# The issue order of all engines, read from a table, in a fused decay-attention and two-MLP kernel

## Chip, cores and metric

One NeuronCore of a Trainium2 chip runs the whole program. The metric is device time in microseconds (us) of one execution, of which the profile's span is the part from the first to the last instruction; durations of single instructions are in nanoseconds (ns).

## What is computed

Inputs are `q`, `k`, `v` of shape (2, 8, 768, 64), one decay `lam` for each of 8 heads, and five weight matrices. The reference, cut to what matters:

```python
for b in range(nb):                                   # blocks of 64 positions
    intra = (qb @ kb.T * Dmask) @ vb
    inter = (qb * lam_pow) @ kv_state
    out[b] = intra + inter
    kv_state = lam**64 * kv_state + (kb * rev_pow).T @ vb
x = out.transpose(0, 2, 1, 3).reshape(1536, 512)
x = (sigmoid(x @ w_gate) * (x @ w_val)) @ w_out       # 512 -> 1536 -> 512
h = x @ w_in                                          # 512 -> 2048
g = where(h > 0, h, exp(min(h, 0)) - 1)
return g @ w_out2                                     # 2048 -> 512
```

## The kernel before

The sequence is cut into 6 chunks of 128 positions. The 1536 tokens stand as columns, in a set of 512 (two chunks of both batches) and one of 1024; the hidden widths are worked off in slices of 256, six of them in the first MLP and eight in the second. Nothing is run in the order of the code: every call on an engine is recorded as an operation (`record`, L167; L182 is the line where all of them are issued later, so every row of the profile has L182), `hazards` (L207) finds which operations must precede which, and `issue` (L408) then chooses one order of all 4713 recorded entries and issues them in it. Each engine runs its own queue strictly in that order and waits on semaphores where a hazard crosses engines.

The order before comes from a list scheduler. `cost` (L140) gives each operation a duration, `run` (L271) simulates the five engines, forwards and backwards, with several settings, and `exchange` (L385) joins the best stages of the orders found; `mark` (L368) sets the stage bounds.

The products are made with operands split in a high and a low part (`h` and `l` in names), three matmuls for each pair of tiles, in fp32r. `product` (L657) makes the 512-row products of a slice in Strassen's manner: seven block products M2, M5, M1, M4, M3, M7, M6 of six matmuls each, in three PSUM banks. M4 and M7 use the first bank one after the other, M3 and M6 the second, so the first matmul of M7 must wait until the result of M4 has been read out of the bank by ScalarE (a sigmoid or an exponential) or VectorE (a multiplication by the gate). The moving operand has 256 columns for the first token set and 512 for the second. `unit` (L996) and `wino_units` (L973) make the output products of a slice in chains in two banks, each followed by an addition into the accumulator by VectorE (`adder`, L1007). `scores` (L788) and the chunk loop make the attention out of groups of small matmuls on 64 by 64 tiles (`together`, L190); the first products of the first MLP are put between these groups.

The profile names a PSUM bank by its first user: `warm` is the bank A0, `direct` B0, `st` one of A1, B1, C0, C1, and `xu` or `x` one of the two banks of the output products. `w` are weights while they are unpacked and split by ScalarE, VectorE and GpSimd.

Of the kernel before, what the change touches and what calls it, by code (L numbers as in the profile page):

```python
# [19 lines left out]
P = 128  # L20
B, H, S, D = 2, 8, 768, 64
# [15 lines left out]
WORDS = 4096  # L37

# [89 lines left out]
class Work:  # L128
# [6 lines left out]
    def __init__(self, nc):  # L135
        self.nc, self.ops, self.block, self.marks = nc, [], None, [0]
        for name in ENGINES:
            setattr(self, name, Engine(self, name))

    def cost(self, op, fn, args, kw):  # L140
# [13 lines left out]
        if fn == "dma_start":  # L154
            return 440, n * P * 4 / 423 if op.eng == "sync" else 2000
# [115 lines left out]
    def run(self, preds, key, backward=False, gate=None, stick=0, thrift=20000):  # L271
        ops = self.ops[::-1] if backward else self.ops
        n = len(ops)
        after, left = [[] for _ in range(n)], [len(p) for p in preds]
        for k, p in enumerate(preds):
            for x in p:
                after[x].append(k)
        ripe, soon = {e: [] for e in ENGINES}, {e: [] for e in ENGINES}
        at, start, end = [max(0.0, g) for g in gate] if gate else [0.0] * n, [0.0] * n, [0.0] * n
        free = dict.fromkeys(ENGINES, 0.0)  # L280
        port = behind = 0.0
        queue = 3500.0
        shape = table = None
        told, pages = 0, {}

        def stall(op, t, keep=False):
            late = 0.0
            here = {}
            for m in range((told + self.FIRST) // self.PAGE, (told + op.words + self.FIRST + self.LEAD) // self.PAGE + 1):
                for mark in (m * self.PAGE - self.FIRST - self.LEAD, m * self.PAGE - self.FIRST):  # L290
                    if m < 2 or not told <= mark < told + op.words:
                        continue
                    now = t + late + op.gap * (mark - told) / op.words
                    if mark == m * self.PAGE - self.FIRST:
                        late += max(0.0, here.get(m, pages.get(m, 0)) - now)
                    else:
                        here[m] = now + (self.SLOW if queue > now + 2000 else self.FAST)
            if keep:
                pages.update(here)
            return late  # L300

        for k in range(n):
            if not left[k]:
                heapq.heappush(soon[ops[k].eng], (at[k], k))
        for _ in range(sum(op.eng is not None for op in ops)):
            t, e = min((free[e] if ripe[e] else max(free[e], soon[e][0][0]), i, e)
                       for i, e in enumerate(ENGINES) if ripe[e] or soon[e])[::2]
            while soon[e] and soon[e][0][0] <= t:
                k = heapq.heappop(soon[e])[1]
                heapq.heappush(ripe[e], (key[k], k))  # L310
            rank, k = heapq.heappop(ripe[e])
            if e == "tensor" and stick and ops[k].shape != shape:
                like = min((x for x in ripe[e] if x[0] < rank + stick and ops[x[1]].shape == shape), default=None)
                if like:
                    ripe[e].remove(like)
                    heapq.heapify(ripe[e])
                    heapq.heappush(ripe[e], (rank, k))
                    k = like[1]
            if e == "tensor" and not backward and thrift and stall(ops[k], t) > 100:
                like = min((x for x in ripe[e] if x[0] < rank + thrift and not stall(ops[x[1]], t)), default=None,  # L320
                           key=lambda x: (ops[x[1]].words, x))
                if like:
                    ripe[e].remove(like)
                    heapq.heapify(ripe[e])
                    heapq.heappush(ripe[e], (rank, k))
                    k = like[1]
            op = ops[k]
            if e == "sync":
                late = 300 if queue < t + 2000 or t < 3000 else 1100
                queue = max(t + 2000, queue) + op.took  # L330
                free[e], end[k] = t + op.gap, queue + late
            elif e == "tensor":
                t += 60 if t > free[e] + 1 else 0
                t += self.SWITCH if op.shape != shape else 0
                shape = op.shape
                late = 0.0
                if not backward:
                    late = stall(op, t, True)
                    told += op.words
                free[e], end[k] = t + late + op.gap, t + late + op.took  # L340
            else:
                if op.table and op.table != table:
                    t, table = t + self.TABLE, op.table
                go = max(t, port, behind if e == "gpsimd" else 0) if op.port else t
                free[e], end[k] = go + op.gap, go + op.took
                if op.port:
                    port = free[e]
                    behind = end[k] + self.HANDOFF["gpsimd"] if e == "vector" else 0
            start[k] = t
            done = [k]  # L350
            while done:
                x = done.pop()
                for s in after[x]:
                    f = ops[s].eng
                    near = e == "tensor" or e == "sync" and (ops[s].prev is op or op.prev is ops[s])
                    ready = free[e] if f == e and x == k and near else end[x] + self.HANDOFF.get(f, 0)
                    at[s] = max(at[s], ready)
                    left[s] -= 1
                    if left[s]:
                        continue  # L360
                    if f is None:
                        start[s] = end[s] = at[s]
                        done.append(s)
                    else:
                        heapq.heappush(soon[f], (at[s], s))
        return start, end

    def mark(self):  # L368
        self.marks.append(len(self.ops))

    def clocks(self, plans):
        work = [sum(op.gap for op in self.ops[:m] if op.eng == "tensor") for m in self.marks[1:]]
        clocks = []
        for start, end in plans:
            order = sorted((start[k], op.gap) for k, op in enumerate(self.ops) if op.eng == "tensor")
            at, done, clock = 0, 0.0, [0.0]
            for w in work:
                while done + order[at][1] <= w:
                    done += order[at][1]
                    at += 1  # L380
                clock.append(order[at][0] + w - done)
            clocks.append(clock + [max(end)])
        return clocks

    def exchange(self, preds, plans, tries=8):  # L385
        bounds = self.marks + [len(self.ops)]
        best = min(plans, key=lambda x: max(x[1]))
        for i in list(range(len(self.marks))) * 2:
            clocks = self.clocks(plans)
            mine = self.clocks([best])[0]  # L390
            ranked = sorted(range(len(plans)), key=lambda r: clocks[r][i + 1] - clocks[r][i])
            for r in ranked[:tries]:
                gain = mine[i + 1] - mine[i] - clocks[r][i + 1] + clocks[r][i]
                if gain <= 0:
                    break
                key = list(best[0])
                for k in range(bounds[i], bounds[i + 1]):
                    key[k] = plans[r][0][k] - clocks[r][i] + mine[i]
                for k in range(bounds[i + 1], len(self.ops)):
                    key[k] -= gain  # L400
                made = self.run(preds, key)
                plans.append(made)
                if max(made[1]) < max(best[1]):
                    best = made
                    mine = self.clocks([best])[0]
        return best

    def issue(self, tc, rounds=7):  # L408
        self.hazards()
        n = len(self.ops)  # L410
        preds = [op.preds for op in self.ops]
        turned = [[] for _ in range(n)]
        for k, p in enumerate(preds):
            for x in p:
                turned[n - 1 - x].append(n - 1 - k)
# [33 lines left out]
def tile_decay_attention_two_mlps(  # L449
# [314 lines left out]
    n = 1  # L764
# [309 lines left out]
    for i in range(1, NG1):  # L1074
# [3 lines left out]
        if i in (2, NG1 - 1):  # L1078
            work.mark()
# [118 lines left out]
```

## Time and profile before

| | before |
|---|---|
| median of 3 runs (lowest, highest) | 581.99 us (581.05, 582.67) |
| the profiled execution's own time | 581.52 us |
| its span, first to last instruction | 579.6 us |
| PE busy | 569.1 us, 98% of the span, 3998 matmuls |
| VectorE busy | 447.8 us, 77%, 771 instructions |
| GpSimd busy | 317.2 us, 55% |
| ScalarE busy | 312.6 us, 54% |
| granted TensorE clock | 0.999 |
| moved by DMA | 52.03 MB, 90 GB/s |

The stages of the span are: to about 71 us the attention with the first products between its groups, to 300 us the first MLP, to 360 us its last slice and the split of its result into the operands of the second, to 520 us the second MLP, and then its last outputs. A row of the timeline gives start, duration, engine, operation and operands; in brackets is the idle time before it and what ended it.

### The profile page before, as it was taken

The page shows a single profiled execution, that of the slowest core. Times are in us where ns is not written, and L with a number is a line of the kernel's source. Part 1 is how long each engine was busy: PE and PEld are TensorE (multiplying, and loading weights), DVE is VectorE, ACT ScalarE, POOL GpSimd, SP SyncE. Part 2 cuts the span into 40 slices and gives each one's busy share as a digit, 9 for nine tenths or more (in the row PEclk, how much of TensorE's full clock was granted, in tenths as well). Part 3 has the DMA queues.
Part 4 walks back from the last instruction along what each step waited for, and adds up shares of the span by engine and source line. Part 5 has one row for each costly group of instructions (what it writes and reads, how often), then busy time and mean ns, then how long its engine had stood idle before and what let it go on. Part 6 is the DMA issues. An engine that isn't in the chain of part 4 may idle for free.

```text
span 579.6 us, 10208 instructions
## 1 busy us (share of the span) xinstructions
PE 569.1 (98%) x3998; PEld 487.2 (84%) x3998; DVE 447.8 (77%) x771; ACT 312.6 (54%) x612; POOL 317.2 (55%) x273
## 2 busy tenths in 40 slices
PE   7899999999999999999999999999999999999997
PEld 4788898888888888888898888888888888888886
DVE  6877844679999989989978994777676667686484
ACT  4893656445345345444457887764746554735160
POOL 2677678875365555553688865574738180712100
PEclk9999999999999999999999999999999999999999
DMA  8946211221221211210140222232222222200014
GB/s 298 411 168 219 75 74 74 74 74 72 74 73 67 80 47 73 98 55 21 72 146 2 74 73 74 72 144 76 73 74 72 74 74 73 74 0 1 0 37 181
DMA packets 10271, 52.03 MB, mean 90 GB/s; under 512 B 1264, under 2 KB 1520, under 8 KB 5744
## 3 DMA queue, kind: packets, MB, share of 16 engines
q1 hardware_dynamic: 10224, 51.39, 24.4%
q8 instruction: 31, 0.51, 0.3%
q14 instruction: 16, 0.13, 0.1%
HBM read 48.24 MB, written 3.15 MB: 89 GB/s over the span
## 4 chain that ended last, share of the span: by engine, by line
PE 89%; ACT 4%; DVE 3%; DMA 3%; issue 1%; SPq 0%; POOL 0%; ACTq 0%; DVEq 0%
PE xu L182 35%; PE st L182 32%; PE direct L182 10%; PE warm L182 9%; PE x L182 2%; DMA w<-in_w_val 1%; DMA w<-in_w_gate 1%; ACT kd L182 1%; ACT w L182 1%; DVE sig L182 1%; DVE sums L182 1%; DVE gl L182 0%; DVE xu L182 0%; ACT sig L182 0%; ACT x143h L182 0%
## 5 line engine op out<-in xcount | busy, mean ns | idle before, releaser
L182 DVE TENSOR_TENSOR acc<-xu,acc 128x512 f32<-128x512 f32 x144 | 96.8, 684 | 21.7 <-PE xu L182 20.9
L182 POOL TENSOR_TENSOR t<-w 128x256 f32<-128x256 f32 (+1 forms) x80 | 69.3, 887 | 70.2 <-DVE w L182 57.6
L182 PE MATMUL xu<-gl,woh 128*128 128x512 f32 (+1 forms) x274 | 107.2, 391 | 0.1
L182 PE MATMUL xu<-gh,woh 128*128 128x512 f32 (+1 forms) x274 | 106.9, 394 | 0.3 <-DVE xt L182 0.2
L182 PE MATMUL xu<-gh,wol 128*128 128x512 f32 (+1 forms) x274 | 106.5, 389 | 0.0
L182 POOL TENSOR_TENSOR wol<-w,woh 128x512 fp32r<-128x512 f32 x34 | 43.4, 1294 | 67.2 <-ACT woh L182 66.5
L182 POOL TENSOR_TENSOR gl<-sig,gh 128x512 fp32r<-128x512 f32 (+1 forms) x30 | 55.0, 1844 | 40.0 <-ACT gh L182 23.9
L182 POOL TENSOR_TENSOR l<-t,h 128x768 fp32r<-128x768 f32 (+1 forms) x38 | 62.6, 1654 | 13.0 <-ACT h L182 4.9
L182 ACT CAST gh<-sig 128x512 fp32r<-128x512 f32 (+1 forms) x66 | 46.7, 714 | 32.5 <-DVE sig L182 31.6
L182 PEld LDWEIGHTS xu<-gh,woh 128*128 128x128 f32 x274 | 51.4, 188 | 11.3 <-DVE xt L182 0.8
L182 PEld LDWEIGHTS xu<-gh,wol 128*128 128x128 f32 x274 | 51.5, 188 | 10.4
L182 PEld LDWEIGHTS xu<-gl,woh 128*128 128x128 f32 x274 | 51.5, 188 | 10.0 <-DVE gl L182 0.5
L182 ACT ACTIVATE sig<-st 128x512 f32<-128x512 f32 (+1 forms) x52 | 29.2, 566 | 53.4 <-PE st L182 35.5
L182 DVE SCALAR_TENSOR_TENSOR w<-w,w 128x1024 uint32<-128x1024 uint32 (+1 forms) x36 | 54.0, 1503 | 0.3
L182 PE MATMUL st<-x143l,h 128*128 128x512 f32 (+1 forms) x150 | 51.8, 347 | 0.0
L182 PE MATMUL st<-x143h,h 128*128 128x512 f32 (+1 forms) x150 | 51.3, 347 | 0.0
L182 PE MATMUL st<-x143h,l 128*128 128x512 f32 (+1 forms) x150 | 50.7, 347 | 0.0
L182 ACT ACTIVATE w<-w 128x1024 f32<-128x1024 f32 (+1 forms) x36 | 39.3, 1092 | 18.0 <-POOL l L182 10.5
L182 DVE TENSOR_SCALAR w<-w 128x1024 uint32<-128x1024 uint32 (+1 forms) x36 | 32.2, 896 | 18.8 <-ACT w L182 18.6
L182 DVE TENSOR_TENSOR wt<-st,wt 128x512 f32<-128x512 f32 (+1 forms) x57 | 31.5, 556 | 14.2 <-PE st L182 13.9
L182 ACT CAST h<-t 128x768 fp32r<-128x768 f32 (+1 forms) x40 | 29.1, 727 | 13.0 <-POOL t L182 12.8
L182 ACT ACTIVATE sig<-sig 128x256 f32<-128x256 f32 (+1 forms) x68 | 34.2, 510 | 1.3
(190 smaller groups left out, 1495.3 us busy)
## 6 DMA issues: line engine op xcount, KB each, us to landing
w<-in_w_out SPq DMA_DIRECT2D x14, 1024.0 KB, 4.8
w<-in_w_in SPq DMA_DIRECT2D x8, 1024.0 KB, 4.8
nat<-in_att SPq DMA_DIRECT2D x12, 512.0 KB, 9.9
w<-in_w_gate SPq DMA_DIRECT2D x5, 1024.0 KB, 4.8
w<-in_w_val SPq DMA_DIRECT2D x5, 1024.0 KB, 4.8
tin<-in_att SPq DMA_DIRECT2D x6, 512.0 KB, 9.7
tin<-in_att SPq DMA_DIRECT2D x3, 1024.0 KB, 11.4
out_t<-o SPq DMA_DIRECT2D x11, 256.0 KB, 2.0
```

Source lines behind the costliest of these rows:

```text
L182: return [getattr(getattr(self.nc, eng), fn)(*(real(a) for a in args), **{k: real(a) for k, a in kw.items()})]
```

## The change

The search leaves the kernel. In its place stands the order that a search elsewhere has found, as a table: one number for each recorded entry, packed as text, from which `order` takes the place of every entry and sorts. It asserts that no entry stands ahead of one that it depends on. The recorded operations, their operands, tiles, buffers and hazards are the same; the two numbers changed in `cost` for a DMA set nothing that is issued any more. Of the 23 KB of table two lines are shown.

```diff
-import heapq
+import base64
 import re
+import zlib
...
+ORDER_TABLE = (
+    'c-qZad2pRqb-(-aZEw?ilAg6$a%4M>qr?u5?O=ywASJOOw6)tp2d0@erDcXv+UdB{q=6yrv>hlNngV~MftJve0FxnGlN3V2V(=u8#WpzgZp*'
...
+    'G<f4Yx4gm=?T3'
+)
...
-            return 440, n * P * 4 / 423 if op.eng == "sync" else 2000
+            return 500, n * P * 4 / 410 if op.eng == "sync" else 2000
...
-    def run(self, preds, key, backward=False, gate=None, stick=0, thrift=20000):
...
-    def exchange(self, preds, plans, tries=8):
...
-    def issue(self, tc, rounds=7):
+    def order(self):
+        raw = np.frombuffer(zlib.decompress(base64.b85decode("".join(ORDER_TABLE))), np.uint8)
+        steps = np.ascontiguousarray(raw.reshape(2, -1).T).view("<i2")[:, 0].astype(int)
+        places = np.cumsum(steps) + np.arange(len(steps))
+        assert len(places) == len(self.ops), "the table is of another program"
+        assert all(places[p] < places[k] for k, op in enumerate(self.ops) for p in op.preds), "an order against a hazard"
+        return np.argsort(places).tolist()
+
+    def issue(self, tc):
         self.hazards()
...
-        order = sorted(range(n), key=lambda k: (best[1][k], k))
+        order = self.order()
```

Counted over the whole program: the 71 transfers stand in the same order on the SP queue. On PE, of 2892 fp32r matmuls, a 512-column one is followed by a 256-column one 129 times where it was 154, and as often the other way round. The small-matmul groups of the attention are entered from, or left to, other matmuls less often: from a group back to fp32r matmuls 14 times where it was 17. Pieces of one product or chain that stand together are 873 where they were 804, and 310 of them are a single matmul where 160 were. VectorE, ScalarE and GpSimd get other orders throughout. Three places follow; before the change a call's line is L182, after it L228, and numbers at names are those of buffers.

PE, early in the attention: `st<-tin` are score groups, `warm<-x11h,h` the first two fp32r matmuls of the first product. Before:

```order
L182 MATMUL st<-tin 64x2x64
L182 MATMUL st<-tin 64x64 x4
L182 MATMUL warm<-x11h,h_180 128x256 x2
L182 MATMUL st<-tin 64x128
L182 MATMUL st<-tin 64x2x64
```

With the change:

```order
L228 MATMUL st<-tin 64x2x64
L228 MATMUL st<-tin 64x64 x4
L228 MATMUL st<-tin 64x128
L228 MATMUL st<-tin 64x2x64
L228 MATMUL st<-tin 64x128
```

The two matmuls of the product have moved behind the second group.

PE, in the third slice of the first MLP, a product of the value weights with 256 columns: M3 in the bank `direct`, then M7 in `warm`, then M6 in `direct` again, which needs the result of M3 read out. Before:

```order
L182 MATMUL direct_494<-x143h0_330,l11_474 128x256
L182 MATMUL warm_80<-xPh0_513,h3_593 128x256
L182 MATMUL warm_80<-xPl0_544,h3_593 128x256
L182 MATMUL warm_80<-xPh0_513,l3_612 128x256
L182 MATMUL warm_80<-xPh0_513,h3_593 128x256
L182 MATMUL warm_80<-xPl0_544,h3_593 128x256
L182 MATMUL warm_80<-xPh0_513,l3_612 128x256
L182 MATMUL st_147<-x143l1_454,h3_593 128x512
L182 MATMUL direct_494<-xPh0_513,h3_593 128x256
```

With the change:

```order
L228 MATMUL direct_516<-x143h0_425,l11_449 128x256
L228 MATMUL warm_79<-xPh0_451,h3_518 128x256
L228 MATMUL warm_79<-xPl0_646,h3_518 128x256
L228 MATMUL warm_79<-xPh0_451,l3_543 128x256
L228 MATMUL warm_79<-xPh0_451,h3_518 128x256
L228 MATMUL warm_79<-xPl0_646,h3_518 128x256
L228 MATMUL warm_79<-xPh0_451,l3_543 128x256
L228 MATMUL direct_516<-xPh0_451,h3_518 128x256
```

The 512-column matmul of another product (`st`) no longer stands between M7 and M6.

VectorE, in the last slice of the first MLP: `sig<-warm,sig` multiplies M7 by the gate and frees the bank `warm` for the next product. Before:

```order
L182 TENSOR_TENSOR sig_1511<-direct,sig_1511 128x256
L182 TENSOR_TENSOR warm<-warm,wt_1042 128x256
L182 TENSOR_SCALAR w_163<-w_163 128x1024
L182 TENSOR_TENSOR xu<-xu,acc_1400 128x512
L182 TENSOR_TENSOR sig_1511<-warm,sig_1511 128x256
```

With the change:

```order
L228 TENSOR_TENSOR xt<-xu,acc_1406 128x256
L228 TENSOR_TENSOR xu<-xu,acc_1406 128x512
L228 TENSOR_TENSOR warm<-warm,wt_1078 128x256
L228 TENSOR_TENSOR sig_1455<-warm,sig_1455 128x256
L228 TENSOR_TENSOR sums<-xu,acc_1406 128x256
```

The unpacking of weights and the addition to `xu` no longer stand between the two steps of M7.

## Rows read from the trace of the kernel before

**Rows 1.** The page: busy us, share of the span, instructions.
```profile
PE 569.1 (98%) x3998; PEld 487.2 (84%) x3998; DVE 447.8 (77%) x771; ACT 312.6 (54%) x612; POOL 317.2 (55%) x273
```
**Rows 2.** Busy time by stage: us, PE, PEld, DVE, ACT, POOL, PEclk, DMA, GB/s.
```profile
90.00:300.00 210.00, 209.90 (x1164) 182.57 (x1163) 183.00 (x279) 95.66 (x167) 124.72 (x111) 1.00 0.20 71
360.00:520.00 160.00, 160.00 (x804) 134.76 (x804) 114.18 (x181) 91.56 (x163) 83.98 (x68) 1.00 0.20 73
```
**Rows 3.** Timeline of PE at 100.7 us: 512-column matmuls, then 256, then 512.
```profile
100.69 0.39 PE L182 MATMUL xu<-gl,woh 128*128 128x512 f32 x1
100.92 0.39 PE L182 MATMUL xu<-gh,wol 128*128 128x512 f32 x1
101.14 0.28 PE L182 MATMUL st<-x143h,h 128*128 128x256 f32 x1
...
103.79 0.28 PE L182 MATMUL direct<-xPh,l 128*128 128x256 f32 x1
103.91 0.40 PE L182 MATMUL st<-x11h,h 128*128 128x512 f32 x1
```
**Rows 4.** Timeline at 316 us: VectorE frees `warm`, PE waits for it.
```profile
316.16 0.41 DVE L182 TENSOR_TENSOR sig<-warm,sig 128x256 f32<-128x256 f32 x1
316.21 0.28 PE L182 MATMUL st<-x143h,h 128*128 128x256 f32 x1
316.62 0.19 PEld L182 LDWEIGHTS warm<-x11h,h 128*128 128x128 f32 x1 [0.34 <-DVE sig L182]
316.63 0.39 PE L182 MATMUL warm<-x11h,h 128*128 128x256 f32 x1
316.85 0.28 PE L182 MATMUL warm<-x11l,h 128*128 128x256 f32 x1
```
**Rows 5.** Timeline at 552 us: a bank freed 0.10 us ahead of its matmul.
```profile
551.25 0.68 DVE L182 SCALAR_TENSOR_TENSOR sig<-sig,st 128x512 f32<-128x512 f32 x1
551.80 0.39 PE L182 MATMUL xu<-gl,woh 128*128 128x512 f32 x1
552.03 0.46 PE L182 MATMUL st<-xPh,h 128*128 128x512 f32 x1
552.33 0.39 PE L182 MATMUL st<-xPl,h 128*128 128x512 f32 x1
```
**Rows 6.** Timeline at 163 us: the place shown of M7 and M6, before.
```profile
162.56 0.42 DVE L182 TENSOR_TENSOR sig<-direct,sig 128x256 f32<-128x256 f32 x1
163.32 0.28 PE L182 MATMUL direct<-xPh,h 128*128 128x256 f32 x1
```
**Rows 7.** Timeline of PE: first and last of 55 late starts behind 71 us.
```profile
71.66 0.35 PE L182 MATMUL warm<-x11h,h 128*128 128x256 f32 x1 [0.50 <-ACT xPh L182]
...
575.73 0.28 PE L182 MATMUL xu<-gl,woh 128*128 128x256 f32 x1
```
**Rows 8.** Groups of VectorE and ScalarE by form: count, busy us, mean ns.
```profile
L182 DVE TENSOR_TENSOR sig<-warm,sig 128x256 f32<-128x256 f32 x16 | 6.7, 419 | 3.8 <-PE warm L182 3.6
L182 ACT ACTIVATE sig<-warm 128x256 f32<-128x256 f32 x34 | 13.1, 384 | 29.7 <-PE warm L182 18.6 <-DVE warm L182 10.8
L182 DVE TENSOR_TENSOR o<-xu,acc 128x512 f32<-128x512 f32 x11 | 7.6, 689 | 4.6 <-PE xu L182 4.6
```
**Rows 9.** Timeline of PE at 14 us: two product matmuls between two score groups.
```profile
13.45 0.90 PE L182 MATMUL st<-tin 64*64 64x128 f32 x32
14.28 0.50 PE L182 MATMUL warm<-x11h,h 128*128 128x256 f32 x2
14.71 0.90 PE L182 MATMUL st<-tin 64*64 64x128 f32 x32
```
**Rows 10.** The tile `w` on VectorE: duration min/median/max ns, first and last start.
```profile
L182 DVE SCALAR_TENSOR_TENSOR w<-w,w x36: 677/1219/3357, 9.8 to 508.3; 128x1024 uint32<-128x1024 uint32 x32, 128x512 uint32<-128x512 uint32 x4
```
**Rows 11.** Timeline at 91 us: VectorE and GpSimd at the same time.
```profile
91.28 3.36 DVE L182 SCALAR_TENSOR_TENSOR w<-w,w 128x1024 uint32<-128x1024 uint32 x1
91.17 2.39 POOL L182 TENSOR_TENSOR gl<-sig,gh 128x1024 fp32r<-128x1024 f32 x1 [0.70 <-DVE w L182]
```

More of the change, by code (lines that the diff above doesn't have):

```diff
@@ L135, in __init__ @@
     def __init__(self, nc):
-        self.nc, self.ops, self.block, self.marks = nc, [], None, [0]
+        self.nc, self.ops, self.block = nc, [], None
         for name in ENGINES:
@@ L269, in hazards @@
             op.preds = sorted(before)
-    def run(self, preds, key, backward=False, gate=None, stick=0, thrift=20000):
[L272 to L383, printed above, removed]
@@ L385, in exchange @@
-    def exchange(self, preds, plans, tries=8):
[L386 to L406, printed above, removed]
@@ L408, in issue @@
-    def issue(self, tc, rounds=7):
-        self.hazards()
[L410 to L415, printed above, removed]
-        best, plans = None, []
-        for stick in (0, 1500, 4000, 10000, 20000):
-            for ahead in (8e3, 20e3):
-                key, gate, least = list(range(n)), None, 1e9
-                for _ in range(rounds):
-                    start, end = self.run(preds, key, gate=gate, stick=stick)
-                    least = min(least, max(end))
-                    plans.append((start, end))
-                    if best is None or max(end) < best[0]:
-                        best = (max(end), start)
-                    _, back = self.run(turned, [-end[n - 1 - k] for k in range(n)], True)
-                    key = [-back[n - 1 - k] for k in range(n)]
-                    gate = ahead and [least + k - ahead for k in key]
-        start, end = self.exchange(preds, plans)
-        best = max(end), start
-        order = sorted(range(n), key=lambda k: (best[1][k], k))
+    def order(self):
[5 more added lines that the diff above has]
+        return np.argsort(places).tolist()
@@ L1077, in tile_decay_attention_two_mlps @@
         last = i + 1 == NG1
-        if i in (2, NG1 - 1):
-            work.mark()
         wG = prep_pair(w_gate, i, nc.gpsimd)
@@ L1111, in tile_decay_attention_two_mlps @@
         last = i + 1 == NG2
-        if i in (2, NG2 - 1):
-            work.mark()
         wH = prep_pair(w_in2, i, nc.gpsimd)
```

41 lines of the change are left out of this document (added).

## The prediction

> **What bounds the kernel now.** I read the page's busy times first [rows 1]: PE is busy for 98% of the span, the next engine, VectorE, for 77%. So PE sets the end, and the same 3998 matmuls will still have to pass through it. Then I read the stages [rows 2]: PE shows 160.00 us busy in the 160 us of the second MLP and 209.90 of 210 in the first. By these two views there is nothing to win. But matmuls overlap in the timeline, and a late one hides in the tail of the one before it, so the third view is the timeline of PE, read from start to start. In an undisturbed stretch a 512-column matmul is followed after 0.23 us, a 256-column one after 0.12 us, although the rows say 0.39 and 0.28 [rows 3]. Every start that comes later than that is time lost, whatever the busy share says.
>
> How such losses come about is seen at 316 us [rows 4]. VectorE frees the bank `warm` at 316.16 + 0.41 = 316.57. The matmul that needs it was due at 316.21 + 0.12 = 316.33; it starts at 316.63, 0.30 late, and the one behind it at 316.85 in place of 316.75, another 0.10. The wait sits on the weight load, not on the matmul. At 552 us [rows 5] the bank is free at 551.25 + 0.68 = 551.93, 0.10 ahead of the matmul due at 552.03: that one starts on time, but the next at 552.33 in place of 552.26, 0.07 late. At 163 us [rows 6] the bank is free at 162.98, 0.34 ahead, and nothing is lost. I call the time from the release to the due start the lead. All three places fit one sum: lost = 0.16 us less the lead, and nothing from 0.16 on (-0.24 gives 0.40; 0.10 gives 0.06). A lead of 0.2 us is enough and one of zero is not.
>
> Read in this way from 71 us to the end, the timeline has 55 matmuls that start over 30 ns late; the first and the last are [rows 7], and together they lose 6.67 us, 1.15% of the span. That, and the way in which the attention's groups are cut, is all that another order of the same work can win or lose on PE.
>
> **The change, part by part.** The recorded work is the same, so nothing is added or removed; only places change.
>
> *Late starts.* At the places where PE now waits the new order has put more between. At 316 us VectorE now goes from the first step of M7 straight to the second; before, 0.68 us of unpacking and an addition of 0.69 us stood between. For the other larger waits (312, 345, 369, 412, 466, 505 us) I counted the matmuls between the last one that feeds the chain and the one that waits, in both orders: the leads grow to 0.43 us or more. I take out all 55: -6.67 us. Between 0 and -6.67 nothing else is possible for this term.
>
> *Short leads by the order itself.* The new order also makes leads shorter, above all in products with 256 columns. At the place shown on PE, M6 follows M3 after six matmuls of M7 and no 512-column one: its first matmul is due 7 x 0.12 = 0.84 us behind the start of the last one of M3. Of that go 0.28 us for this matmul, 0.04 for the handover and 0.42 for VectorE's multiplication [rows 8], so the lead is 0.10 us and 0.06 us is lost. Where ScalarE reads the bank, 0.38 us [rows 8], the lead is 0.14 and 0.02 us is lost. Counted over both orders with these durations, behind 71 us there are 30 such places (11 before), 28 of them with 256 columns, 20 read by ScalarE and 10 by VectorE, losing 38 ns in the mean: 30 x 0.038 = +1.15 us. It can hardly be less, since the reading engine is taken to be free; what it may be more stands in the last term. The Trainium skill, "TensorE: Matmul & The Clock Gate", section "Step-by-step: what each phase is for", says that PE pulls weight loads ahead of matmuls in flight, so that the next weights load while the present matmul runs. By that alone a result that is there ahead of its matmul would cost nothing, and the sum would be 1.15 us lower. The trace does not agree where the load itself has to wait: [rows 5] lose 0.07 us with the result 0.10 us early.
>
> *The last units.* One chain's last matmul moves behind three matmuls of the next, so that the chain two further on finds its bank late: 4 x 0.23 - 0.39 - 0.04 - 0.69 [rows 8] = -0.21 us of lead, +0.37 us. In return the very last chain, which now loses 0.34 us (among the 55), starts behind that delay and should lose nothing.
>
> *Attention.* PE goes from a small-matmul group back to products 14 times, not 17. Two product matmuls between two score groups take 14.71 - 14.28 = 0.43 us [rows 9], where two in a stream take 0.24: 0.19 us for each going out and back. Three: -0.6 us. As ends I take 0 and double that. The other waits of the first 71 us, for transfers and for single steps of the scores, I take as unchanged, since the SP queue and what the attention computes from chunk to chunk stay as they are; I allow them 1 us either way.
>
> *Size changes.* 25 fewer pairs of changes between 512 and 256 columns. From 512 to 256 the starts are 0.22 us apart, from 256 to 512 0.12 [rows 3], the same as without a change. So this is worth nothing, and no cover is needed.
>
> *Late starts that no count shows.* A count that takes the reading engine to be free finds only 11 short leads in the order before, where the trace has 55 late starts and 6.67 us: most come from engines that were not free. The new order will have its own of these. The first MLP has 0.72 us of late starts in 210 us, the second 1.59 in 160 (6 and 18 of the 55). At the first rate the 508 us behind 71 us give 1.7 us, at both stages' joint rate of 2.32 in 370, 3.2 us. I take the middle, +2.4; the ends are 0 and, as badly as now, 6.67.
>
> The sum is made against the profiled execution's own 581.52 us: 581.52 - 6.67 + 1.15 + 0.37 - 0.6 + 2.4 = 578.2. The median of the runs, 581.99, is 0.47 above that execution, so for a median I add as much: **578.6 us**.
>
> **Rivals.**
>
> *The order holds as planned*: the uncounted late starts stay near zero. For it speaks that the now waiting places all get longer leads, and that the first MLP, with VectorE at its fullest, has the fewest late starts now, 0.72 us in 210, so that a full VectorE need not make PE wait. Against it: 30 leads that have no slack at all. 578.6 - 2.4 = 576.2 us.
>
> *Waits change places*: as many uncounted late starts as now. For it: VectorE is busy for 183 of 210 us in the first MLP [rows 2], so that it often stands in another instruction when a bank is ready, and a short lead leaves no time for that. 581.52 + 1.15 + 0.37 - 0.6 + 0.47 = 582.9 us, no change that can be told.
>
> *Slower, by VectorE held up ahead of a short lead.* The unpacking on VectorE takes 1.22 us in the middle and up to 3.36 [rows 10]; the longest stands beside a GpSimd subtraction that runs through most of it [rows 11]. A multiplication that must free a bank within 0.1 us of slack, queued behind such an instruction, comes up to 2.14 us late, and all of PE behind it. Before, 512-column matmuls in between took a part of that up; at the 30 places they are gone. At half of 2.14 for each, seven of the places hit cost 7.5 us: 586.1 us. It decides from five hits on (5.35 us), which take 578.6 past 583.7. Against it: at 20 of the 30 places ScalarE reads the bank, and the orders of VectorE and GpSimd were moved as well. The Trainium skill, "SBUF — State Buffer", section "Terms", has a rule for this: VectorE and GpSimd share a pair of ports under an exclusive lock, and the loser is blocked fully. The trace agrees [rows 11].
>
> That the order is not what its description says is so in part: products stand in more pieces than before, not fewer. It changes no number, since pieces cost nothing by [rows 3].
>
> **How the numbers follow.** Forecast 0.59, order holds 0.12, waits change places 0.20, slower 0.09. A measurement of this kernel tells some 0.3% from no change, 1.75 us: faster is below 580.2, slower above 583.7. The forecast's own ends (uncounted waits from 1.7 us to what the second MLP's rate gives, 1.59 / 160 x 508 = 5.0) are 577.9 and 581.2, so some 0.08 of its chance lies in the middle band. Faster 0.12 + 0.51 = 0.63, same 0.20 + 0.08 = 0.28, slower 0.09. The range runs from just below the first rival to just short of the second, of which it leaves out about half, and the third: 575.9 to 582.7.
>
> **What will show it.** In the changed profile: late starts behind 71 us of some 3.9 us in sum, most of them single ones of 20 to 70 ns in 256-column products; VectorE's multiplication directly followed by an undelayed start at 316 us; one late start of 0.3 to 0.4 us three units from the end and none at the last; PE's first fp32r matmuls behind the fourth score group of the first two chunks. It is wrong if the sum of late starts stays at 6 us or more, or if starts over 0.5 us late stand behind VectorE's unpacking.

## The result: 575.54 us, and the profile after

The changed kernel takes **575.54 us** in the median of 4 runs (575.05 to 576.78), the kernel before 582.0 beside it: a ratio of 0.9893, with a 95% interval of 0.9872 to 0.9915, a gain of 6.46 us. The forecast was 578.6: the direction is right, the gain is nearly twice the forecast, and the time lies 0.36 us under the low end of the range. The profiled execution took 575.05 us, its span 573.3.

The page of the changed kernel answers to [rows 1], with busy us, share of the span and instructions:

```profile
PE 564.8 (99%) x3997; PEld 488.2 (85%) x3998; DVE 441.2 (77%) x771; ACT 316.4 (55%) x612; POOL 313.9 (55%) x273
```

and the stages to [rows 2] (us, PE, PEld, DVE, ACT, POOL, PEclk, DMA, GB/s):

```profile
90.00:300.00 210.00, 210.00 (x1153) 182.76 (x1153) 176.39 (x286) 99.99 (x173) 123.74 (x113) 1.00 0.21 76
360.00:520.00 160.00, 160.00 (x822) 136.78 (x821) 113.55 (x176) 89.74 (x161) 84.24 (x68) 1.00 0.20 73
```

Neither tells where the gain is. (One matmul record is missing, 3997 for 3998.) VectorE is nearly as full as before. PE's busy time fell by 4.3 us with the same work, because part of a late matmul's wait stands in its own duration: 0.39 us at 316.63 in [rows 4], where 0.28 is usual. The starts tell. At the place of [rows 4], the timeline of VectorE and PE in the changed kernel:

```profile
313.94 0.43 DVE L228 TENSOR_TENSOR warm<-warm,wt 128x256 f32<-128x256 f32 x1
314.40 0.42 DVE L228 TENSOR_TENSOR sig<-warm,sig 128x256 f32<-128x256 f32 x1
314.75 0.42 DVE L228 TENSOR_TENSOR sums<-xu,acc 128x256 f32<-128x256 f32 x1
315.05 0.27 PE L228 MATMUL direct<-xPl,h 128*128 128x256 f32 x1
315.16 0.28 PE L228 MATMUL warm<-x11h,h 128*128 128x256 f32 x1
315.28 0.28 PE L228 MATMUL warm<-x11l,h 128*128 128x256 f32 x1
```

The bank is free at 314.40 + 0.42 = 314.82, the matmul is due at 315.17: 0.35 us of lead, and the starts are 0.11 and 0.12 apart. The place of [rows 6], from which the prediction worked out a lead of 0.10 us:

```profile
161.27 0.42 DVE L228 TENSOR_TENSOR sig<-direct,sig 128x256 f32<-128x256 f32 x1 [0.35 <-PE direct L228]
161.67 0.28 PE L228 MATMUL warm<-xPh,l 128*128 128x256 f32 x1
161.78 0.35 PE L228 MATMUL direct<-xPh,h 128*128 128x256 f32 x1
161.97 0.28 PE L228 MATMUL direct<-xPl,h 128*128 128x256 f32 x1
```

Free at 161.69, due at 161.67 + 0.12 = 161.79, and the next start comes at 161.97 in place of 161.90. Lead and loss are the forecast ones, 0.10 and about 0.06. The last units, answering to the end of [rows 7]:

```profile
568.00 0.39 PE L228 MATMUL xu<-gh,wol 128*128 128x512 f32 x1
568.49 0.39 PE L228 MATMUL xu<-gh,woh 128*128 128x256 f32 x1
568.72 0.28 PE L228 MATMUL xu<-gl,woh 128*128 128x256 f32 x1
...
569.79 0.28 PE L228 MATMUL xu<-gl,woh 128*128 128x256 f32 x1
569.91 0.28 PE L228 MATMUL xu<-gh,wol 128*128 128x256 f32 x1
```

568.49 is 0.26 us late and 568.72 another 0.11, 0.37 as forecast; at the very end no start is late.

Summed over PE's timeline (a start that comes over 30 ns later than 0.227 us behind a 512-column matmul or 0.120 behind a 256-column one), the late starts are, as count / us:

| kernel | 71 to 90 us | 90 to 300 | 300 to 360 | 360 to 520 | 520 to end |
|---|---|---|---|---|---|
| before | 9 / 1.59 | 6 / 0.72 | 18 / 2.28 | 18 / 1.59 | 4 / 0.48 |
| changed | 2 / 0.16 | 10 / 0.62 | 4 / 0.27 | 4 / 0.34 | 2 / 0.37 |

55 late starts with 6.67 us became 22 with 1.76. That is 4.91 of the 6.30 us by which the span fell. The other 1.39 are put down to the first 71 us, as what is left; they hold starts under 30 ns late too.

### The profile page after: what moved, and what is told of

Its sections match the earlier page's. It is cut to its first block, busy times and chain, and to the rows that moved or that the text cites. A ratio compares the mean times of both kernels' runs of the same rounds, so it can differ in the third digit from the quotient of the medians.

```text
span 573.3 us, 10166 instructions
## 1 busy us (share of the span) xinstructions
PE 564.8 (99%) x3997; PEld 488.2 (85%) x3998; DVE 441.2 (77%) x771; ACT 316.4 (55%) x612; POOL 313.9 (55%) x273
## 4 chain that ended last, share of the span: by engine, by line
PE 93%; DMA 3%; DVE 2%; ACT 1%; issue 0%; SPq 0%; DVEq 0%
PE xu L228 37%; PE st L228 34%; PE direct L228 11%; PE warm L228 10%; PE x L228 2%; DMA nat<-in_att 1%; DMA w<-in_w_gate 1%; SPq L228 0%; DVE w L228 0%; ACT L228 0%; DVE o L228 0%; DVE sig L228 0%; DVE pr L228 0%; ACT kd L228 0%; ACT sig L228 0%
## 5 line engine op out<-in xcount | busy, mean ns | idle before, releaser
L228 DVE TENSOR_TENSOR acc<-xu,acc 128x512 f32<-128x512 f32 x144 | 97.8, 686 | 31.2 <-PE xu L228 30.5
L228 POOL TENSOR_TENSOR t<-w 128x256 f32<-128x256 f32 (+1 forms) x80 | 69.5, 886 | 86.0 <-DVE w L228 53.7
L228 PE MATMUL xu<-gl,woh 128*128 128x512 f32 (+1 forms) x274 | 106.5, 389 | 0.0
L228 PE MATMUL xu<-gh,woh 128*128 128x512 f32 (+1 forms) x274 | 106.0, 390 | 0.1
L228 PE MATMUL xu<-gh,wol 128*128 128x512 f32 (+1 forms) x274 | 105.2, 389 | 0.0
L228 POOL TENSOR_TENSOR gl<-sig,gh 128x512 fp32r<-128x512 f32 (+1 forms) x30 | 54.3, 1816 | 64.8 <-ACT gh L228 53.8
L228 ACT CAST gh<-sig 128x512 fp32r<-128x512 f32 (+1 forms) x66 | 46.5, 712 | 56.7 <-PE xu L228 28.7
L228 POOL TENSOR_TENSOR l<-t,h 128x768 fp32r<-128x768 f32 (+1 forms) x38 | 60.8, 1604 | 13.9 <-DVE w L228 6.8
L228 POOL TENSOR_TENSOR wol<-w,woh 128x512 fp32r<-128x512 f32 x34 | 43.7, 1294 | 33.3 <-ACT woh L228 28.5
L228 PEld LDWEIGHTS xu<-gh,woh 128*128 128x128 f32 x274 | 51.5, 188 | 11.6 <-DVE o L228 0.5
L228 PEld LDWEIGHTS xu<-gh,wol 128*128 128x128 f32 x274 | 51.5, 188 | 10.4
L228 PEld LDWEIGHTS xu<-gl,woh 128*128 128x128 f32 x274 | 51.5, 188 | 9.3 <-POOL gl L228 0.2
L228 PE MATMUL st<-x143l,h 128*128 128x512 f32 (+1 forms) x150 | 51.9, 347 | 0.0
L228 DVE SCALAR_TENSOR_TENSOR w<-w,w 128x1024 uint32<-128x1024 uint32 (+1 forms) x36 | 51.5, 1434 | 0.2
L228 PE MATMUL st<-x143h,h 128*128 128x512 f32 (+1 forms) x150 | 51.6, 347 | 0.0
L228 PE MATMUL st<-x143h,l 128*128 128x512 f32 (+1 forms) x150 | 51.3, 347 | 0.0
L228 ACT ACTIVATE sig<-st 128x512 f32<-128x512 f32 (+1 forms) x52 | 29.2, 564 | 35.9 <-DVE st L228 23.5
L228 ACT ACTIVATE w<-w 128x1024 f32<-128x1024 f32 (+1 forms) x36 | 39.3, 1093 | 15.8 <-POOL l L228 5.5
L228 DVE TENSOR_TENSOR wt<-st,wt 128x512 f32<-128x512 f32 (+1 forms) x57 | 31.9, 560 | 12.7 <-PE st L228 8.3
L228 DVE TENSOR_SCALAR w<-w 128x1024 uint32<-128x1024 uint32 (+1 forms) x36 | 33.0, 919 | 10.8 <-ACT w L228 10.3
L228 ACT CAST h<-t 128x768 fp32r<-128x768 f32 (+1 forms) x40 | 28.9, 726 | 13.3 <-POOL t L228 13.2
L228 ACT ACTIVATE sig<-sig 128x256 f32<-128x256 f32 (+1 forms) x68 | 33.9, 507 | 1.5
```

The lines of the kernel that those rows point to most:

```text
L228: return [getattr(getattr(self.nc, eng), fn)(*(real(a) for a in args), **{k: real(a) for k, a in kw.items()})]
```

## The experiments

Theory A: stage by stage the time is what start to start gives, and at each place lost = 0.16 us less the lead; the new order leaves hardly any place short. The main rivals: the orders of the readers (the engines that read a bank out and free it) would do it alone; a lead above zero costs nothing; size changes cost.

**Head alone, end alone.** Only the numbers of the table differ, as in all other runs but the two with `MOVES`; where that tells more, a place of the order is shown instead:

```diff
 ORDER_TABLE = (
-    'c-qZad2pRqb-(-aZEw?ilAg6$a%4M>qr?u5?O=ywASJOOw6)tp2d0@erDcXv+UdB{q=6yrv>hlNngV~MftJve0FxnGlN3V2V(=u8#WpzgZp*'
+    'c-qZad5oP^6~FuPZEu}7OJ_QT(oXl5md#Q&0}_N3QHT)5h%t&$6QaSy^$!ta)EMv&<AR!KzzPDQfJQ6|Et@TkluDtUwzh?KTH2XTXJ6j?Jont!'
...
```

> Everything that the changed kernel issues up to 70 us stands in the changed order, all that is left in the order before (the two orders have done the same PE work, but for one 256-column matmul, at 70.0 us of the one trace and 71.0 us of the other). Theory A, the gain is the sum of separate stages: 1.1 us of it belongs to this stretch, so 580.9 us against 582.0 before. By the prediction's own term for the attention (0.6 us) it would be 581.4. Rival, the new head shifts the engines against each other and by that also clears late starts far behind it: 578 us or less. If the boundary itself costs, over 582.

> Everything up to 212 us in the order before, the rest in the changed order. Theory A: the changed trace is 2.2 us ahead at 240 us and 6.3 at the end, so 4.1 us lie behind the cut; the count of the late starts alone gives 3.6. So 577.9 to 578.4 us. Rival, the late starts of the second MLP went because of what the engines had done long before: a gain under 2.5 us, 579.5 or more.

The head alone: 581.61 us against 582.18, ratio 0.999 (0.998 to 1.0001). The first 70 us are worth 0.6 us with an interval from -0.1 to 1.2, which holds the prediction's term and theory A's 1.1 alike, but not the rival. Its trace has 0.95 us fewer late starts between 71 and 90 us than the kernel before, so some of the late starts right behind the cut come from the attention ahead of it. The end alone: 577.70, ratio 0.9929 (0.9917 to 0.9941), 4.1 us (3.4 to 4.8). Theory A's 3.6 to 4.1 came; its late starts behind 71 us are 2.85 us where before has 6.67, and its span fell by 3.7. So the end's gain needs nothing of the new beginning. The stretch from 70 to 212 us was not run alone.

**The readers' order alone.** PE's order is that of before, word for word. On GpSimd, one of the moves of the first run, as rows of its queue:

```diff
-TENSOR_TENSOR wol_1190<-w_163,woh_1151 128x512
 TENSOR_TENSOR x143l_454<-sums,x143h_184 128x6x128
+TENSOR_TENSOR wol_1194<-w_163,woh_1152 128x512
```

> The order before on PE and SP, word for word; on VectorE 49, on ScalarE 41 and on GpSimd 11 instructions stand in another place, so that what frees a bank for a waiting matmul stands ahead of other work wherever that helps. Theory A, the order on PE sets the leads and bunches what the readers must do: the count with the durations of the rows gives 4.8 us of late starts in place of 6.3, so 1.5 us less, 580.5 us. Rival, the late starts come from readers that stand in other work, and PE's order matters little: most of the 4.9 us by which late starts fell, 577 to 578 us.

> As the run with the readers' order alone, but everything up to 122 us stands as before, and PE's order is that of before throughout: 40 instructions on VectorE, 34 on ScalarE and 9 on GpSimd in other places. Theory A, PE's order sets how short the leads are: 1.4 us of late starts go by the count, 580.6 us, or less goes, since the run before it had 4.99 us of late starts behind 90 us where the kernel before has 5.08. Rival, the readers' places matter most: 3.5 us or more go, under 578.5 us. Under 580 us in either case the run before it was slow through its start alone.

The first of the two took 588.07 us, ratio 1.0105 (1.009 to 1.012), and neither theory had that. The timeline of GpSimd and PE shows that the move above was a bad one:

```profile
74.06 1.81 POOL L225 TENSOR_TENSOR x143l<-sums,x143h 128x768 fp32r<-128x768 f32 x1 [3.79 <-ACT x143h L225]
75.83 1.26 POOL L225 TENSOR_TENSOR wol<-w,woh 128x512 fp32r<-128x512 f32 x1
77.14 0.50 PE L225 MATMUL st<-gh,wol 128*128 128x512 f32 x1 [2.79 <-POOL wol L225]
```

`wol`, which PE needs, now stood behind `x143l`, for whose operand GpSimd waited 3.79 us; PE then waited 2.79 for `wol`. One place, about half of the loss. With the start left as before, the second run gives 581.74 us, ratio 0.9997 (0.9988 to 1.0005): nothing. Its late starts behind 90 us are 5.05 us, before's 5.08; 0.7 went between 360 and 520 us, and as much came between 300 and 360. So 83 instructions in other places on the readers bring nothing without PE's order. The count's 1.4 us did not come either; "or less" did. These are orders chosen by the count, not the changed kernel's own, and the new order of PE with the readers as before was not run: how the gain divides between PE and its readers stays open.

**VectorE's neighbours.** Behind the sort in `order` (14 pairs; three shown):

```diff
+MOVES = (
+    (840, 832), (1098, 1094), (1352, 1365),
...
+)
-        return np.argsort(places).tolist()
+        order = np.argsort(places).tolist()
+        for what, ahead in MOVES:
+            order.remove(what)
+            order.insert(order.index(ahead), what)
```

> The changed kernel with 14 swaps of two neighbours on VectorE, of its 771 instructions, over 20 us apart from each other: an instruction that frees a bank or makes an operand for PE now stands behind its neighbour, which is 0.41 to 1.22 us long. Theory A, lost = 0.16 us less the lead at each: the sum is 8.7 us, 575.5 + 8.7 = 284 + 300.2 = 584.2 us. Rival 1, a result that is there ahead of its matmul costs nothing (the 0.16 is not there): 14 x 0.16 less, 582.0 us. Rival 2, PE has slack again behind each place and most is made good: under 579 us, and the prediction's uncounted late starts would be rare by themselves, not by this order.

(The sum in that text is 575.5 + 8.7; the "284 + 300.2" is a slip.) Measured: 587.35 us, ratio 1.0093 (1.008 to 1.0106), 11.8 above the changed kernel and not 8.7, so that theory A's sum was missed. Read place by place against the changed kernel's trace, 10 of the 14 cost what was counted to within 0.1 us, 6.38 against 6.35 in sum; without the 0.16 at each it would be 4.75, and rival 1 falls. The other four cost 4.76 against 2.39. The largest of them, and behind the dots another, in the timeline of VectorE, GpSimd and PE:

```profile
176.63 1.82 DVE L233 TENSOR_TENSOR gl<-sig,gh 128x512 fp32r<-128x512 f32 x1
178.37 0.68 DVE L233 TENSOR_TENSOR sig<-st,sig 128x512 f32<-128x512 f32 x1
176.05 1.85 POOL L233 TENSOR_TENSOR l<-t,h 128x768 fp32r<-128x768 f32 x1
179.10 0.50 PE L233 MATMUL st<-x22h,h 128*128 128x512 f32 x1 [1.31 <-DVE sig L233]
...
426.48 0.74 POOL L233 TENSOR_TENSOR t<-w 128x256 f32<-128x256 f32 x1 [0.76 <-DVE gl L233]
426.64 1.13 DVE L233 TENSOR_TENSOR gl<-sig,gh 128x512 fp32r<-128x512 f32 x1 [0.31 <-ACT gh L233]
```

The neighbour `gl`, 0.69 us in the median of the changed kernel's trace, takes 1.82 beside GpSimd's subtraction, and the bank-freeing `sig` behind it comes that much later. This is the prediction's third rival at one place: a hold-up of VectorE by GpSimd, passed on to PE. At 426.64 us another `gl` takes 1.13 us in the same way; the two are stretched by 1.6 us in sum. The unpacking that was put ahead at 364 and at 400 us took its usual 1.23 and 1.21 us, so the excess is not GpSimd's throughout. The Trainium skill, "SBUF — State Buffer", section "Terms", states the exclusive port for these two engines, the loser blocked in full. The trace agrees: both `gl` end 0.55 us behind the GpSimd instruction (last section). Rival 2, slack behind each place, falls.

**Leads on PE.** The same code with 23 pairs of matmuls:

```diff
+MOVES = (
+    (805, 824), (1165, 1156), (1253, 1184), (1298, 1293),
...
```

> The changed kernel with 23 swaps of two neighbouring matmuls on PE, over 11 us apart from each other: a matmul that waits for a reader's result is issued one place earlier, ahead of a matmul that waits for nothing (14 with 256 columns, 9 with 512). Theory A, lost = 0.16 us less the lead: 0.11 to 0.15 us at each, 2.9 us in all, 578.4 us. Rival, a result that is there ahead of its matmul costs nothing, as weight loads are pulled ahead: the leads stay above zero at nearly all places, 0.2 us in all, 575.7 us.

Measured: 579.85 us, ratio 0.9964 (0.9949 to 0.9978), 4.3 above the changed kernel and 1.45 above theory A's sum. At the 23 places the two traces differ by 3.10 us in sum, where 2.92 were counted. The trace is of an execution of 581.53 us, and another 3.2 us of its excess lie in the first 70 us, which the edit leaves alone (last section). The place at 161 us, shown above, in this kernel:

```profile
164.78 0.42 DVE L234 TENSOR_TENSOR sig<-direct,sig 128x256 f32<-128x256 f32 x1 [0.36 <-PE direct L234]
165.06 0.28 PE L234 MATMUL warm<-xPl,h 128*128 128x256 f32 x1
165.26 0.39 PE L234 MATMUL direct<-xPh,h 128*128 128x256 f32 x1
165.48 0.28 PE L234 MATMUL warm<-xPh,l 128*128 128x256 f32 x1
```

Free at 165.20, due at 165.18: a lead of -0.02, and 0.08 + 0.10 = 0.18 us lost. The Trainium skill, "TensorE: Matmul & The Clock Gate", section "Step-by-step: what each phase is for", lets weight loads run ahead; by that alone the run would have cost 0.2 us. The trace does not agree where the load has to wait for a reader's result.

**Size changes.** More pairs of changes than the changed kernel's 129, by single matmuls moved on PE. They are 251 by PE's rows, not the 272 of the text below; the first place:

```diff
 MATMUL st<-gh_1340,wol_1186 128x512
+MATMUL direct<-x143h_425,h_179 128x256
 MATMUL st<-x22h_701,l_609 128x512
+MATMUL direct<-x143l_509,h_179 128x256
 MATMUL st<-x22h_701,h_564 128x512
-MATMUL st<-x22l_733,h_564 128x512
 MATMUL warm<-xPh_451,h_320 128x256
+MATMUL st<-x22l_733,h_564 128x512
```

> The changed kernel with 143 more pairs of changes between 512 and 256 columns on PE (272 in place of 129), made by moving single matmuls up to 16 places, so that no lead gets shorter than 0.16 us that was not; the other engines' orders are the same. Theory A, a change of size costs nothing: 575.5 us, within 0.5. Rival, each change costs PE something that starts in an undisturbed stretch don't show, 20 ns or more: 286 x 0.02 = 5.7, over 581 us.

Measured: 577.54 us, ratio 0.9927 (0.9913 to 0.9941), which is neither theory A's 575.5 within 0.5 nor the rival's 581. The trace, of an execution of 576.43 us, is 1.4 us longer than the changed kernel's, 0.7 of it behind 70 us. A stretch of PE's timeline:

```profile
152.19 0.28 PE L227 MATMUL direct<-xPl,h 128*128 128x256 f32 x1
152.31 0.40 PE L227 MATMUL st<-x143h,l 128*128 128x512 f32 x1
152.55 0.28 PE L227 MATMUL direct<-xPh,l 128*128 128x256 f32 x1
152.67 0.39 PE L227 MATMUL st<-x143h,h 128*128 128x512 f32 x1
152.90 0.27 PE L227 MATMUL direct<-xPh,h 128*128 128x256 f32 x1
```

Over the whole trace a start 256 behind 512 comes after 233.5 ns (512 behind 512: 228.2), one 512 behind 256 after 118.0 (256 behind 256: 119.5): 4 ns for a pair, 0.5 us for the 122 pairs more. The 25 pairs that the change saves are worth 0.1 us. The rival's 20 ns for each change fall; "nothing" was right to that much. The other 0.7 us of the trace lie in the head; where the rest up to 577.54 is lost is not shown.

**Fewer short leads.** Two orders with which the count of lost time falls further. The first moves instructions on all engines; one of them on ScalarE:

```diff
+CAST woh_1141<-w_168 128x1024
 ACTIVATE sig_391<-direct 128x256
 ACTIVATE sig_391<-sig_391 128x256
 ACTIVATE sig_1455<-st 128x512
 ACTIVATE sig_1455<-sig_1455 128x512
-CAST woh_1141<-w_168 128x1024
```

> The changed kernel with some 40 moves by a few places on all engines, chosen by the rule lost = 0.16 us less the lead alone: late starts behind 71 us by the rule 0.5 us in place of 1.7, PE's order the same otherwise. Theory A: 575.5 - 1.2 = 574.3 us, faster than both kernels. Rival, moves bring new delays that the rule does not know (VectorE stretched beside GpSimd, as in the run with the 14 swaps): 575.5 us or more.

Measured: 578.51 us, ratio 0.9934 (0.992 to 0.9948). The rival came. The timeline of VectorE, GpSimd, ScalarE and PE at 374 us shows the worst move:

```profile
371.82 2.75 DVE L227 SCALAR_TENSOR_TENSOR w<-w,w 128x1024 uint32<-128x1024 uint32 x1
371.64 1.85 POOL L227 TENSOR_TENSOR l<-t,h 128x768 fp32r<-128x768 f32 x1 [0.63 <-DVE w L227]
374.60 1.05 ACT L227 CAST woh<-w 128x1024 fp32r<-128x1024 f32 x1 [2.73 <-DVE w L227]
375.56 0.37 ACT L227 ACTIVATE sig<-direct 128x256 f32<-128x256 f32 x1
376.89 0.39 PE L227 MATMUL direct<-x11h,h 128*128 128x256 f32 x1 [0.17 <-DVE sig L227]
```

The cast of the weights now waits 2.73 us for the unpacking, which takes 2.75 us beside GpSimd; the read of `direct` stands behind it and PE behind that. Between 376 and 381 us PE has 1.75 us of late starts, the changed kernel none.

The second moves matmuls on PE alone, and the changed kernel ran again beside it. One of the 30 moves, ahead of a product that waits for its bank:

```diff
+MATMUL st<-x143h_184,h_468 128x512
 MATMUL direct<-xPh_451,h_320 128x256
 MATMUL direct<-xPl_646,h_320 128x256
...
-MATMUL st<-x143h_184,h_468 128x512
```

> The changed kernel with 30 single matmuls that wait for nothing brought, on PE alone and behind 90 us, ahead of a matmul that waits; VectorE, ScalarE, GpSimd and SP keep their orders word for word. Theory A, with the other engines left alone the rule lost = 0.16 us less the lead holds: 1.06 us of late starts go (1.6 behind 90 us in the trace of the changed kernel), so 0.5 to 0.7 are left, and the time is 1.1 us under that of the changed kernel in the same runs. Rival, PE's order and the readers' order fit only each other, and any move brings new late starts, as in the run with moves on all engines: 1.6 us of late starts or more.

> The changed kernel itself once more, beside the run below. If the 575.5 us hold, 575.0 to 576.8, then the 1.8 to 3 us by which three variants came out above the sum (their traces show part of that in the first 60 us, which their edits leave as they are) belong to the variants. If it gives 577 or more, the first 60 us differ from one run to the next, and a gain of 1 us can be read only from the late starts of the trace.

Measured: 575.57 us against 576.14 for the changed kernel in the same runs (0.9897, 0.9882 to 0.9911; and 0.9901, 0.9887 to 0.9914). No difference can be told, and the trace has 1.66 us of late starts behind 90 us, the changed kernel 1.60 and 1.53 in its two traces. The rival came: eleven of the changed kernel's late starts are gone and eleven others have come. No version here beats the changed kernel measurably. The changed kernel itself, 576.14 us where it first had 575.54, stays within the 575.0 to 576.8 of the text: the larger excess of the three variants is theirs, though their edits leave the first 60 us alone.

## Why the prediction was right, and where it failed

- **The 55 late starts.** They were all taken out. Of the larger ones named (312, 316, 345, 369, 412, 466, 505 us) none is left. Right.
- **The law of the lead.** Over eleven of the traces there are 460 places behind 72 us with a lead between -1.0 and 0.16 us. In bins of the lead, lost time plus lead is 157 to 164 ns in the median of every bin; at some 150 places with 160 to 200 ns of lead the loss is 2 ns in the median. Three places gave the right sum.
- **Short leads by the order itself, last units.** Forecast 1.15 + 0.37 = 1.52 us at 30 places and in the last units. Behind 72 us the changed trace has 43 places with a lead under 0.16 us. At 32 of them the reading engine began within 0.1 us of having its operand, as the count takes it; they lose 1.36 us, of which the last units have 0.37. The count was right.
- **Late starts that no count shows: the step that failed.** The prediction added 2.4 us, a rate taken from the stages of the kernel before. The late starts behind 71 us were to be 3.9 us and are 1.76; beside the 1.52 that leaves 0.24 for the term. That sum leaves out what is under 30 ns. With it taken in, the other 11 of the 43 places, where the reading engine came later, lose 0.91 us; the kernel before, read in the same way, has 33 such places with 4.59 us. So the term was 1.5 to 2.2 us too large, and the time came out near the rival "the order holds as planned" (576.2 us), held at 0.12. The runs show what is wrong in the step. Uncounted late starts do not come at a rate that a full VectorE sets: VectorE is nearly as full as before, 176 of 210 us and 114 of 160, and they have fallen to a fifth. They sit at single places where a reader's queue has another instruction in front. Fourteen swaps among VectorE's 771 instructions brought 11 us of them, and the run with the end alone has 1.25 us behind 90 us after an old beginning. Such places can be counted if each reader's queue is walked through with its durations. Done afterwards, with each operation's shortest duration in the two traces, this gives 1.7 us for the changed order and 6.3 for the one before. An estimate of the same kind needs the trace before alone: with the median duration of each form there, the walk from 74 us on gives 1.4 us for the changed order and 5.1 for the one before, where the traces lose 2.2 and 5.9; the difference is right. With each single instruction's duration from the trace before it gives over 15 for the changed order: there the instructions that GpSimd held up are others, and a stretched duration belongs to its place, not to its form.
- **Attention.** The place of [rows 9] in the changed kernel's timeline:

```profile
14.47 2.08 PE L228 MATMUL st<-tin 64*64 64x128 f32 x64
16.49 0.50 PE L228 MATMUL warm<-x11h,h 128*128 128x256 f32 x2
```

  Two score groups stand together, and the products come behind them, as said. Forecast -0.6. The two traces differ by 1.39 us there, the run with the head alone by 0.6 (-0.1 to 1.2). Up to 0.8 us too small, within the 1 us allowed for other waits. The second trace of the changed kernel, with a span of 574.3 us and 1.79 us of late starts, leaves 0.4 us for the same stretch, so how much of it is lasting stays open (last section).
- **Size changes.** Forecast 0, measured 0.1 us.
- **Slower, by VectorE held up.** The mechanism is real (two hold-ups of 1.6 us among the swaps, and ScalarE waited 2.73 at one place of the order with fewer short leads), but the table does not put such an instruction ahead of a short lead: from 71 us to the last units no start in its trace is over 0.11 us late. What speaks against it in the prediction, that VectorE's order was moved as well, is what the swaps bear out.

The two sums: 2.2 us from the uncounted term and 0.8 from the head make up the 3.0 us between 578.6 and 575.5. The first holds in both traces of the changed kernel (1.76 and 1.79 us of late starts). The second is in part the scatter of the head, and so is the side of the range's end on which the median falls: 575.54 is 0.36 us below it, 576.14 inside.

## What to carry to other kernels

With PE at 98% busy, read it from start to start: the late starts held 4.9 of the 6.3 us, and one law, 0.16 us less the lead, prices each of them. If another order is to be judged, count the leads with every reader's queue walked through, using undisturbed durations, in place of carrying a rate over from the old order; and mark where a two-operand VectorE instruction falls beside a GpSimd one. An order also sets waits of its own here: in both kernels `issue` lets each GpSimd instruction with two operands in SBUF wait for the VectorE instruction using the shared port that was issued last ahead of it ([rows 11]: 0.70 us for `w`), so such a walk has to carry them. Small rearrangements of a finished order, of the readers alone or of single instructions that a count favours, gave nothing or lost.

## What the runs showed of the hardware

- The 0.16 us have two parts. With a lead above 0.06 us the waiting matmul itself is on time (-2 to 4 ns in the bins from 0.04 us on) and only the next one is late; below that the next is late by a steady 102 to 109 ns and the waiting one by the rest.
- How long GpSimd holds VectorE up can be worked out. Where a `gl` subtraction of 128x512 (0.69 us in the median) starts while a GpSimd instruction runs and is stretched, it ends 0.54 to 0.56 us behind that instruction's end, at all 169 places of the twelve traces; the unpacking `w` of 128x1024 (1.22 us) ends 1.08 to 1.09 us behind it at all 96. [rows 11] and the rows at 176 and 372 us above show it.
- The first 70 us, issued in the same order, differ by up to 3 us between the changed kernel and its variants, and by 1.0 us between the two traces of the changed kernel itself. In the kernel with 23 swapped matmuls, which stands as the changed one there, the timeline of PE and the stretches behind it (columns as in [rows 2]) show:

```profile
55.75 0.88 PE L234 MATMUL x<-ql,sn 64*64 64x128 f32 x22
58.12 0.65 PE L234 MATMUL x<-ql,sn 64*64 64x128 f32 x10 [1.50 <-issue]
...
60.15 0.41 PE L234 MATMUL warm<-x143l,h 128*128 128x256 f32 x1
60.36 0.41 PE L234 MATMUL warm<-x143h,l 128*128 128x256 f32 x1
```

```profile
50.00:60.00 10.00, 8.50 (x185) 7.62 (x185) 4.08 (x12) 3.96 (x8) 4.11 (x3) 0.95 0.40 144
60.00:70.00 10.00, 9.77 (x141) 8.88 (x141) 6.59 (x17) 6.61 (x18) 8.05 (x6) 0.88 0.31 107
```

PE stops for 1.50 us in the middle of a group of small matmuls, and nothing that the profile shows holds it. Behind that the granted clock falls, to 0.88 in the mean of ten us, and 256-column matmuls start 0.21 us apart in place of 0.12, the lower of the two clock levels. That trace is 3.2 us behind the changed kernel's at 70 us. What makes PE stop was not tried. One thing in the traces points at the fetching of instructions: a 16 KB packet of the queue `q8 instruction` lands at 56.67 us, where PE has just stopped (55.75 + 0.88 = 56.63), while in the changed kernel's trace the corresponding packet landed at 53.88, some 120 of PE's instructions earlier, and PE ran on. That the late packet is the cause is not shown.
